# Causal attention with beacons, then a ReGLU FFN, on one core: scores issued three packed slabs at a time, output stores on another queue, block loads ordered behind the transpose of x

## The chip, the core and the metric

The kernel runs on one core of one Trainium2 chip. A core has five engines that run side by side and wait for each other through semaphores: TensorE (PE, matmuls; its weight loads are shown apart as PEld), VectorE (DVE), ScalarE (ACT), GpSimd (POOL) and SyncE (SP), which here issues DMAs. SP, ACT and POOL each have a queue of instructions in order; a DMA issued from a queue waits in it like any other instruction. The metric is the device time of one execution in microseconds (us). The kernel before takes 378.92 us, the median of 4 runs (378.21 to 380.38).

## The reference

```python
B, H, S, Nb, D = 8, 8, 576, 16, 64            # batches, heads, tokens, beacons, head width
k_all = concatenate([beacon_k, k], axis=2)    # 592 keys
v_all = concatenate([beacon_v, v], axis=2)
scores = (1 / sqrt(D)) * matmul(q, k_all.transpose(0, 1, 3, 2))
scores = where(causal, -1e9, scores)          # beacons are seen by all, tokens causally
a = exp(scores - scores.max(-1)); a /= a.sum(-1) + 1e-09
x = matmul(a, v_all)                          # then laid out as 4608 tokens x 512
gate, val = maximum(x @ w_gate, 0), x @ w_val # 512 -> 1536
out = (gate * val) @ w_out                    # 1536 -> 512
```

All inputs and the output are float32; the kernel computes in bfloat16 with float32 sums. It leaves out the maximum in the softmax (a flag computed at the end sends inputs out of range to a slow general path, which does not run with these inputs).

## The kernel before, in words

**Attention.** Keys are the partitions of a score tile, queries its columns. The 592 keys are five blocks of up to 128 rows (`kt`), and the queries fall into two groups: the first 368 rows (group 0) and the other 208 (group 1). The unit of work is a *burst*: one batch, one pair of heads (each head takes 64 of the 128 rows of PE, so two matmuls run side by side) and one query group. A batch has 4 x 2 = 8 bursts. The table `SLABS` lists, for each group, two *slabs* of up to 512 columns a head: which key block against which queries goes to which column. A slab is computed into one PSUM tile `s` of two banks, one bank a head; the pool `s_ps` has two such tiles.

A burst goes through `qk` (L331; the score matmuls, L339), `softmax` (L343; exp on ACT, L347, from PSUM to a bfloat16 tile `p`), `mask` (L350; DVE multiplies the diagonal part by a triangle, L358) and, one tick later, `av` (L360; the P·V matmuls, L378, whose last column gives the row sums; DVE normalises into `x`, L386 and L387). After the last head pair of a group, `x_turn` (L391) transposes x into `xT` by three or two DMAs on SP (L394).

**FFN.** `ffn_up` (L407) makes one 128-row slice of the hidden layer for one tile of tokens (368 or 208 wide): four gate matmuls (L411), relu on ACT (L414), four value matmuls (L417), the product on DVE (L425). `ffn_down` (L429) makes 128 rows of the output: twelve matmuls of 512 columns (L448), a copy by ACT to one of three output buffers `ob` (L451), and the store (L453). All PSUM tiles but the scores come from `f_ps`, a ring of four banks given out strictly in turn; the tile that takes a bank waits until its former content was read.

**Loads.** For batches 2 to 7 a `Load` fetches one block of k and q, or two blocks of v, into one of six staging buffers (DMAs on SP), POOL casts it to bfloat16 (L269, L282), and two DMA transposes on SP (L296) bring k and q to `kq`. `kq` and `vx` exist twice, for even and odd batches.

**Order.** It is written out by hand, and each engine runs its instructions in that order. After a start for batch 0, the loop of L657 goes through *ticks*, one burst of batches 1 to 7 in each (L633). A tick emits the burst's scores and exps, P·V of the burst of the tick before and, after a last head pair, the turn of x; then the casts and transposes of blocks loaded two and three ticks ago, the next block's load, and the masks. Then as many FFN pieces follow as a budget allows (L647): `ffn` is a list of pieces with an estimated cost in PE time, and `ready` says from which tick the x of a piece is there. Where the next piece is a narrow up (cost under 1) the second exp is placed after the first piece. Pieces left after the last tick follow at the end (L694).

Of the kernel before, what the change touches and what calls it, by code (L numbers as in the profile page):

```python
# [10 lines left out]
FP32 = mybir.dt.float32  # L11
# [131 lines left out]
def kernel(  # L143
# [15 lines left out]
    P = 128  # L159
# [169 lines left out]
        pass  # L329

    def qk(u):  # L331
        u.s, u.p = [], []
        kq = kqs[u.b % 2]
        for segs, cols, _ in SLABS[u.g]:
            s = s_ps.tile([P, 2, 512], FP32, name="s")
            for (kt, q0, n, c) in segs:
                for a in range(2):
                    rows = slice(a * D, (a + 1) * D)
                    T.matmul(s[:, a, c:c + n], kq[rows, 0, u.pi, kt * P:(kt + 1) * P],  # L339
                             kq[rows, 1, u.pi, Nb + q0:Nb + q0 + n], start=True, stop=True)  # L340
            u.s.append(s)

    def softmax(u, which=(0, 1)):  # L343
        for i in which:
            cols = SLABS[u.g][i][1]
            p = psb.tile([P, 2, 512], BF16, name="p")
            A.activation(p[:, :, :cols], u.s[i][:, :, :cols], AF.Exp, scale=scale)  # L347
            u.p.append(p)

    def mask(u, pool=False, which=(0, 1)):  # L350
        for i in which:
# [8 lines left out]
    def av(u):  # L360
        qt = QGROUPS[u.g]
        o = f_ps.tile([P, len(qt), 2, D + 2], FP32, name="f")
        blocks = {}
        for p, (segs, cols, _) in zip(u.p, SLABS[u.g]):
            for (kt, q0, n, c) in segs:
                for j, qi in enumerate(qt):
                    r0, rn = QROWS[qi]
                    if q0 <= r0 and r0 + rn <= q0 + n:
                        blocks[j, kt] = (p, c + r0 - q0)
        first = True  # L370
        for j, qi in enumerate(qt):
            kts = sorted(kt for (jj, kt) in blocks if jj == j)
            m = 80 if qi == 4 else P
            for a in range(2):
                for kt in kts:
                    p, c = blocks[j, kt]
                    kr = P if kt < 4 else KT4
                    T.matmul(o[:m, j, a, 0:D + 1], p[:kr, a, c:c + m],  # L378
                             vs[u.b % 2][:kr, kt, 2 * u.pi + a, 0:D + 1],
                             start=first, stop=(kt == kts[-1]), skip_group_check=True)  # L380
                    first = False
        parts = ((0, 3, P),) if u.g == 0 else ((0, 1, P), (1, 2, 80))
        for j0, j1, m in parts:
            i0 = qt[j0]
            r = rall[:m, u.b, u.pi, i0:i0 + j1 - j0]
            V.reciprocal(r, o[:m, j0:j1, :, D])  # L386
            V.tensor_mul(  # L387
                u.x[:m, i0:i0 + j1 - j0, u.pi * P:(u.pi + 1) * P].rearrange("p j (a d) -> p j a d", a=2),
                o[:m, j0:j1, :, 0:D], r.unsqueeze(3).to_broadcast([m, j1 - j0, 2, D]))
# [15 lines left out]
    hbs = {}  # L405

    def ffn_up(m0, mn, nf):  # L407
        def go():
            g = f_ps.tile([P, 512], FP32, name="f")
            for ki in range(KM):  # L410
                T.matmul(g[:, :mn], wg[:, ki, nf * P:(nf + 1) * P], xT[:, ki, m0:m0 + mn],  # L411
                         start=(ki == 0), stop=(ki == KM - 1))
            gs = fsb.tile([P, 512], FP32, name="g")
            A.activation(gs[:, :mn], g[:, :mn], AF.Relu)  # L414
            u = f_ps.tile([P, 512], FP32, name="f")
            for ki in range(KM):
                T.matmul(u[:, :mn], wv[:, ki, nf * P:(nf + 1) * P], xT[:, ki, m0:m0 + mn],  # L417
                         start=(ki == 0), stop=(ki == KM - 1))
            c = m0
            while c < m0 + mn:  # L420
                i = c // HB
                e = min((i + 1) * HB, m0 + mn)
                if i not in hbs:
                    hbs[i] = fsb.tile([P, NF, HB], BF16, name="hT")
                V.tensor_mul(hbs[i][:, nf, c - i * HB:e - i * HB], gs[:, c - m0:e - m0], u[:, c - m0:e - m0])  # L425
                c = e
        return go

    def ffn_down(i, ms):  # L429
        rows = slice(i * HB + ms * P, i * HB + (ms + 1) * P)  # L430

        def last():
            for n0 in (0, 256):
                o = f_ps.tile([P, 256], FP32, name="f")
                for nf in range(NF):
                    T.matmul(o, hbs[i][:, nf, ms * P:(ms + 1) * P], wo[:, nf, n0:n0 + 256],  # L436
                             start=(nf == 0), stop=(nf == NF - 1))
                ob = osb_p.tile([P, 256], FP32, name="ob")
                A.copy(ob, o)
                (A if n0 else nc.sync).dma_start(out[rows, n0:n0 + 256], ob)  # L440

        if (i + 1) * HB == n_tokens and ms == HB // P - 1:
            return last

        def go():
            o = f_ps.tile([P, d_model], FP32, name="f")
            for nf in range(NF):
                T.matmul(o, hbs[i][:, nf, ms * P:(ms + 1) * P], wo[:, nf, :],  # L448
                         start=(nf == 0), stop=(nf == NF - 1))
            ob = osb_p.tile([P, d_model], FP32, name="ob")  # L450
            A.copy(ob, o)  # L451
            oq = nc.sync if len(ffn) < 8 else OQ
            oq.dma_start(out[rows], ob)  # L453
        return go
# [14 lines left out]
        T.matmul(cnt_ps, ok, ones, start=True, stop=True)  # L469
        V.tensor_copy(cnt, cnt_ps)  # L470

    OQ = nc.sync
    NA, PRE = 2, 16
    tiles = []
    for b in range(B):
# [2 lines left out]
    with tc.manual_schedule():  # L478
# [13 lines left out]
        for b in range(B):  # L492
            for p, g in [(p, g) for g in range(2) for p in range(NP)]:
                u = Burst()
                u.b, u.pi, u.g, u.last = b, p, g, p == NP - 1
                bursts.append(u)

        def start(u):
# [76 lines left out]
                ffn += [(2.6, ffn_down(done, ms), m0 + mn) for ms in range(HB // P)]  # L575
                done += 1

        def next_ffn():
            ffn.pop(0)[1]()

        def burst(u):
            start(u)
# [45 lines left out]
        for b in range(2, B):  # L628
            kq = [Load("kq", b, t) for t in range(NKT)]
            vv = [Load("v", b, t, min(t + 2, NKT)) for t in range(0, NKT, 2)]  # L630
            pieces += [(b, x) for x in (kq[0], vv[0], kq[1], kq[2], vv[1], kq[3], kq[4], vv[2])]
        T0, GAP = 8, 1
        ticks = bursts[8:16] + [None] * GAP + bursts[16:] + [None]  # L633
        begin = {b: T0 + GAP + 8 * (b - 1) for b in range(2, B)}

        ready = {}
        for m0, mn in tiles:
            e = m0 + mn
            if e <= S:
                ready[e] = 0  # L640
                continue
            for s, u in enumerate(ticks, T0):
                if u and u.last and u.b * S + (368 if u.g == 0 else S) >= e:
                    ready[e] = s + 3
                    break

        def budget(s):  # L647
            best = 4.6 if s >= T0 + 8 else 2.4
            for r in sorted(set(ready.values())):
                if r > s:  # L650
                    best = min(best, sum(c for c, _, e in ffn if ready[e] < r) / (r - s))
            return best

        jobs = []
        prev = None
        spent, want = 0.0, 0.0
        for s, u in enumerate(ticks, T0):  # L657
            turn = u and u.b == 1 and u.g == 0 and not u.last
            if turn:
                pair_turn(c1, 1, u.pi + 1, 2, VA)  # L660
            late = False
            if u:
                late = not turn and ffn and ready[ffn[0][2]] <= s and ffn[0][0] < 1
                start(u)
                qk(u)
                softmax(u, (0,) if late else (0, 1))
            if prev:
                av(prev)
                if prev.last:
                    x_turn(prev)  # L670
            for at, f in [j for j in jobs if j[0] == s]:
                f()
            for _ in range(1):
                if pieces and s >= begin[pieces[0][0]] - 10:
                    b, x = pieces.pop(0)
                    x.issue()
                    jobs.append((s + 2, lambda x=x: x.cast(G)))
                    if x.kind == "kq":
                        jobs.append((s + 3, lambda x=x: x.turn()))
            rest = []  # L680
            if late:
                rest = [lambda: (softmax(u, (1,)), mask(u, which=(0,))), lambda: mask(u, which=(1,))]
            elif u:
                mask(u)
            prev = u
            want += budget(s)
            while ffn and ready[ffn[0][2]] <= s and spent + ffn[0][0] / 2 <= want:
                spent += ffn[0][0]
                next_ffn()
                if rest:  # L690
                    rest.pop(0)()
            for f in rest:
                f()
        while ffn:  # L694
            if len(ffn) == 10:
                range_flags()
# [38 lines left out]
```

## Time and profile before

| | us |
|---|---|
| median of 4 runs (lowest to highest) | 378.92 (378.21 to 380.38) |
| the profiled execution | 380.84 |
| its span, first to last instruction | 379.1 |
| PE busy, share of the span | 362.7, 96% |
| ACT busy | 204.7, 54% |
| DVE busy | 188.3, 50% |
| POOL busy | 73.0, 19% |
| granted PE clock, mean | 0.995 |

In rows of the profile, `f<-xT,wg` is an instruction that writes tile f from xT and wg; then come its shape, the count, and what it waited for. "SPq" is a DMA issued on the queue of SP. A time in brackets with an arrow is idle time of that engine before the instruction, and what ended it.

### The profile page before, as it was taken

Reading aid. Unit: us, or ns where it says so; the run is one execution under the profiler, and the core shown is the slowest. Engines: PE = TensorE matmul, PEld = TensorE weight load, DVE = VectorE, ACT = ScalarE, POOL = GpSimd, SP = SyncE. Lnnn points to the kernel's source line nnn. Section 1 sums busy time; section 2 is a strip of 40 time slices with the busy share of each in tenths; the row PEclk is TensorE's granted clock in tenths of the full one; section 3 lists DMA queues with packets and bytes.
Section 4 is the critical chain, followed back from the end, with each engine's and each line's share of the span. In section 5 each row is a group of like instructions: output and inputs, shape, how many; then the busy total and the mean of one; then the engine's idle time right before and its main releaser. Section 6 shows DMA issues by size and latency. Waiting matters only on the chain.

```text
span 379.1 us, 9589 instructions
## 1 busy us (share of the span) xinstructions
PE 362.7 (96%) x3757; PEld 237.3 (63%) x3757; DVE 188.3 (50%) x642; ACT 204.7 (54%) x372; POOL 73.0 (19%) x94
## 2 busy tenths in 40 slices
PE   2889998999999999999999999999999999999995
PEld 1547666567756686565596647865596647765763
DVE  3747458456635674265256633565165633552230
ACT  4755367546556665455465545565466545642321
POOL 5952023212221212121303122121202000000000
PEclk9989999999999999999999999999999999999999
DMA  8999999999989999898977496778959212001202
GB/s 145 178 200 207 179 208 176 192 188 119 175 158 216 131 153 163 201 166 143 220 123 158 87 228 150 133 134 149 210 100 162 42 55 84 15 14 39 85 31 88
DMA packets 158995, 53.12 MB, mean 140 GB/s; under 512 B 146528, under 2 KB 154464, under 8 KB 158944
## 3 DMA queue, kind: packets, MB, share of 16 engines
q1 hardware_dynamic: 149840, 45.24, 63.4%
q0 software_dynamic: 8816, 6.88, 11.9%
q8 instruction: 31, 0.51, 0.6%
q10 hardware_dynamic: 288, 0.33, 0.3%
q14 instruction: 20, 0.16, 0.2%
HBM read 38.47 MB, written 9.44 MB: 126 GB/s over the span
## 4 chain that ended last, share of the span: by engine, by line
PE 91%; DMA 3%; POOL 2%; ACT 1%; DVE 1%; issue 1%; DVEq 0%; ACTq 0%
PE f L417 24%; PE f L448 24%; PE f L411 24%; PE f L378 10%; PE s L339 7%; DMA wv<-in_moe_w_val_dram 2%; DMA stg<-in_k_dram 1%; ACT p L347 1%; PE f L436 1%; PE f L322 1%; POOL p L355 1%; DVE hT L425 0%; POOL cs L308 0%; POOL wg L507 0%; DVE p L358 0%
## 5 line engine op out<-in xcount | busy, mean ns | idle before, releaser
L425 DVE TENSOR_TENSOR hT<-g,f 128x208 bf16<-128x208 f32 (+14 forms) x288 | 92.8, 350 | 79.8 <-PE f L417 48.6
L417 PE MATMUL f<-xT,wv 128*128 128x368 bf16 (+1 forms) x768 | 126.1, 287 | 1.0 <-DMA wv<-in_moe_w_val_dram 0.5
L411 PE MATMUL f<-xT,wg 128*128 128x368 bf16 (+1 forms) x768 | 125.7, 286 | 1.0 <-ACT g L414 0.5
L414 ACT ACTIVATE g<-f 128x368 f32<-128x368 f32 (+1 forms) x192 | 78.9, 413 | 73.6 <-PE f L411 35.5
L347 ACT ACTIVATE p<-s 128x992 bf16<-128x992 f32 (+2 forms) x128 | 105.5, 864 | 19.9 <-PE s L339 19.8
L448 PE MATMUL f<-wo,hT 128*128 128x512 bf16 x420 | 94.3, 379 | 0.1
L417 PEld LDWEIGHTS <-wv 128*128 128x128 bf16 x768 | 71.4, 98 | 26.0 <-issue 0.9
L411 PEld LDWEIGHTS <-wg 128*128 128x128 bf16 x768 | 69.5, 98 | 21.2 <-issue 1.4
L448 PEld LDWEIGHTS <-hT 128*128 128x128 bf16 x420 | 40.1, 98 | 44.7
L282 POOL CAST c<-stg 128x1024 bf16<-128x1024 f32 (+1 forms) x30 | 31.9, 1063 | 133.1 <-DMA stg<-in_q_dram 133.1
L451 ACT COPY ob<-f 128x512 f32<-128x512 f32 x35 | 20.5, 585 | 67.5 <-PE f L448 66.2
L386 DVE RECIPROCAL rall<-f 128x2 f32<-128x2 f32 (+1 forms) x96 | 16.7, 174 | 76.9 <-PE f L378 76.4
L378 PEld LDWEIGHTS <-p 128*128 128x128 bf16 (+2 forms) x960 | 37.3, 108 | 13.7 <-issue 12.0
L378 PE MATMUL f<-vx,p 128*128 128x65 bf16 (+2 forms) x960 | 44.2, 200 | 0.8 <-DVE p L358 0.8
L358 DVE TENSOR_TENSOR p<-p,tri 128x160 bf16<-128x160 bf16 (+1 forms) x124 | 40.6, 346 | 4.5 <-ACT p L347 4.1
L387 DVE TENSOR_TENSOR x<-f,rall 128x128 bf16<-128x128 f32 (+1 forms) x96 | 36.3, 378 | 3.4
L339 PE MATMUL s<-kq 64*128 64x208 bf16 (+4 forms) x512 | 35.8, 261 | 1.8 <-ACT p L347 1.5
L269 POOL CAST vx<-stg 128x1024 bf16<-128x1024 f32 (+2 forms) x21 | 18.9, 898 | 76.1 <-DMA stg<-in_v_dram 73.9
L339 PEld LDWEIGHTS <-kq 64*128 64x128 bf16 x512 | 17.0, 97 | 19.5 <-issue 18.7
L325 DVE COPY kq<-f 128x192 bf16<-128x192 bf16 (+2 forms) x18 | 8.5, 507 | 5.3 <-PE f L322 4.6
L319 PE MATMUL f<-ident,c 64*128 64x64 bf16 x12 | 0.5, 234 | 6.3 <-DVE c L279 6.3
L322 PEld LDWEIGHTS <-cs 64*64 64x64 bf16 x264 | 3.6, 120 | 3.7 <-issue 3.6
(50 smaller groups left out, 53.6 us busy)
## 6 DMA issues: line engine op xcount, KB each, us to landing
out_dram<-ob SPq DMA_DIRECT2D x35, 256.0 KB, 3.3
stg<-in_v_dram SPq DMA_DIRECT2D x24, 256.0 KB, 4.6
stg<-in_k_dram SPq DMA_DIRECT2D x18, 256.0 KB, 3.9
stg<-in_q_dram SPq DMA_DIRECT2D x18, 256.0 KB, 4.2
stg<-in_v_dram SPq DMA_DIRECT2D x8, 224.0 KB, 3.4
wo<-in_moe_w_out_dram POOLq DMA_DIRECT2D x3, 512.0 KB, 14.5
stg<-in_k_dram SPq DMA_DIRECT2D x6, 224.0 KB, 3.7
stg<-in_q_dram SPq DMA_DIRECT2D x6, 224.0 KB, 3.7
```

Source lines behind the costliest of these rows:

```text
L282: cp(self.c[:n], self.st[:n])
L339: T.matmul(s[:, a, c:c + n], kq[rows, 0, u.pi, kt * P:(kt + 1) * P], kq[rows, 1, u.pi, Nb + q0:Nb + q0 + n], start=True, stop=True)
L347: A.activation(p[:, :, :cols], u.s[i][:, :, :cols], AF.Exp, scale=scale)
L358: V.tensor_mul(p[:, :, :m], p[:, :, :m], tri[:, :, :m])
L378: T.matmul(o[:m, j, a, 0:D + 1], p[:kr, a, c:c + m], vs[u.b % 2][:kr, kt, 2 * u.pi + a, 0:D + 1], start=first, stop=(kt == kts[-1]), skip_ ...
L387: V.tensor_mul(u.x[:m, i0:i0 + j1 - j0, u.pi * P:(u.pi + 1) * P].rearrange("p j (a d) -> p j a d", a=2), o[:m, j0:j1, :, 0:D], r.unsqueeze ...
L411: T.matmul(g[:, :mn], wg[:, ki, nf * P:(nf + 1) * P], xT[:, ki, m0:m0 + mn], start=(ki == 0), stop=(ki == KM - 1))
L414: A.activation(gs[:, :mn], g[:, :mn], AF.Relu)
L417: T.matmul(u[:, :mn], wv[:, ki, nf * P:(nf + 1) * P], xT[:, ki, m0:m0 + mn], start=(ki == 0), stop=(ki == KM - 1))
L425: V.tensor_mul(hbs[i][:, nf, c - i * HB:e - i * HB], gs[:, c - m0:e - m0], u[:, c - m0:e - m0])
L448: T.matmul(o, hbs[i][:, nf, ms * P:(ms + 1) * P], wo[:, nf, :], start=(nf == 0), stop=(nf == NF - 1))
L451: A.copy(ob, o)
```

## The change

Batch 0 and batch 1 keep their order. From batch 2 on, the ticks are replaced by 28 *phases* (in the code, a step that is a list). A batch's 8 bursts are cut into 14 slabs in place of 16: of two bursts of group 0, the two short second slabs (256 columns each) are packed into one of 512. A phase takes three slabs, across bursts and batches. Their scores are issued together at its start: the first slab into two tiles of the FFN ring `f_ps` (on loan, one bank a head, each with an exp of its own), the other two into `s_ps`. The first slab's exp follows at once, then one P·V whose last slab was in the phase before. The other exps are placed inside FFN pieces (`mid`, between relu and the value matmuls of an up, or between the matmuls and the copy of a down), at least 1.2 us of estimated PE time apart, and after such a piece comes another P·V that is due; a mask follows one FFN piece after its exp.

A phase counts as 3 x 8/14 = 1.71 ticks. Loads, casts and transposes have due times on that clock and are emitted between FFN pieces as it passes, but not while P·V of a last head pair is still to come in the phase (`held`), so that the turn of x stands before them on SP. The stores of the output, all but those of the last pieces, are issued by POOL in place of SP (`OQ`).

```diff
+    class Slab:
+        def __init__(self, segs, cols, spans):
+            self.segs, self.cols, self.spans = segs, cols, spans
+        def qk(self, s):
+            self.s = s
+            for u, (kt, q0, n, c) in self.segs:
+                kq = kqs[u.b % 2]
+                for a in range(2):
+                    rows = slice(a * D, (a + 1) * D)
+                    o = s[a] if isinstance(s, list) else s[:, a]
+                    T.matmul(o[:, c:c + n], kq[rows, 0, u.pi, kt * P:(kt + 1) * P],
+                             kq[rows, 1, u.pi, Nb + q0:Nb + q0 + n], start=True, stop=True)
+        def exp(self):
+            p = self.p = psb.tile([P, 2, 512], BF16, name="p")
+            if isinstance(self.s, list):
+                for a in range(2):
+                    A.activation(p[:, a, :self.cols], self.s[a][:, :self.cols], AF.Exp, scale=scale)
+            else:
+                A.activation(p[:, :, :self.cols], self.s[:, :, :self.cols], AF.Exp, scale=scale)
+            for u, seg in self.segs:
+                u.parts.append((p, (seg,)))
...
     def ffn_up(m0, mn, nf):
-        def go():
+        def go(mid=None):
...
             A.activation(gs[:, :mn], g[:, :mn], AF.Relu)
+            if mid:
+                mid()
             u = f_ps.tile([P, 512], FP32, name="f")
...
-    OQ = nc.sync
+    OQ = G
...
-        ticks = bursts[8:16] + [None] * GAP + bursts[16:] + [None]
+        steps = bursts[8:16] + [None] * GAP + bursts[16:8 + NT]
+        steps += [slabs[i:i + 3] for i in range(0, len(slabs), 3)] + [None]
+        widths = [W * len(e) if isinstance(e, list) else 1 for e in steps]
...
+            for i, sl in enumerate(e):
+                for u, _ in sl.segs:
+                    start(u)
+                sl.qk([f_ps.tile([P, 512], FP32, name="f") for _ in range(2)] if i == 0 else
+                      s_ps.tile([P, 2, 512], FP32, name="s"))
+            exps, masks = list(e), []
...
+            exp()
+            aver()
+            if not held():
+                passed(pos[s])
+            gone, was, room = 0.0, spent, max(want - spent, 0.1)
+            while fits():
+                c = ffn[0][0]
+                gone += c
+                mid = gone >= STEP
+                if mid:
+                    gone = 0.0
+                old = len(masks)
+                next_ffn(exp if mid else None)
+                spent += c
+                if old:
+                    masks.pop(0).mask()
+                if mid:
+                    aver()
+                if not held():
+                    passed(pos[s] + widths[s] * min((spent - was) / room, 0.99))
+            while exps:
+                exp()
+            while units:
+                aver()
+            for sl in masks:
+                sl.mask()
```

Here `exp()` takes the next slab of the phase and `aver()` the next P·V that is due, with the turn of x where it is the last; `passed(t)` emits the loads, casts and transposes due by t. The FFN may take 5.2 us of PE per tick's width where the limit was 4.6.

## The prediction

> **What bounds the kernel now.** I read the page first: busy time of each engine over the span.
>
> ```profile
> span 379.1 us, 9589 instructions
> PE 362.7 (96%) x3757; PEld 237.3 (63%) x3757; DVE 188.3 (50%) x642; ACT 204.7 (54%) x372; POOL 73.0 (19%) x94
> ```
>
> TensorE (PE) is busy for all but 16.4 us, and no other engine is above 54%. The second view, busy time by stretch, says where those 16.4 us lie (columns: stretch, length, then busy us of PE, weight loads, DVE, ACT and POOL with their instruction counts, then granted clock, DMA share and GB/s).
>
> ```profile
> 0.00:20.00 20.00, 11.56 (x184) 8.14 (x185) 10.44 (x29) 11.94 (x20) 14.30 (x30) 1.00 1.05 163
> 60.00:80.00 20.00, 19.20 (x228) 12.26 (x226) 12.93 (x42) 13.03 (x22) 5.42 (x5) 1.00 1.09 188
> 160.00:180.00 20.00, 20.00 (x185) 11.86 (x184) 11.54 (x42) 11.38 (x20) 3.73 (x4) 1.00 0.94 165
> 360.00:379.10 19.10, 14.39 (x102) 9.27 (x100) 3.15 (x10) 4.31 (x11) 0.00 (x0) 1.00 0.17 59
> ```
>
> Idle PE is in the start (before 80 us) and after the last matmul. From 80 to 360 us each stretch has 20.00 of 20.00. Batches 2 to 7 run there, and only for them does the change rewrite the order.
>
> Busy is not the same as streaming, so the third view is PE in order of time, where starts can be subtracted (start, duration, engine, line, operation, count).
>
> ```profile
> 78.45 0.79 PE L417 MATMUL f<-xT,wv 128*128 128x368 bf16 x4
> 79.07 0.79 PE L378 MATMUL f<-vx,p 128*128 128x65 bf16 x18
> 79.69 0.79 PE L411 MATMUL f<-xT,wg 128*128 128x368 bf16 x4
> ...
> 164.49 0.79 PE L417 MATMUL f<-xT,wv 128*128 128x368 bf16 x4
> 165.21 0.49 PE L339 MATMUL s<-kq 64*128 64x128 bf16 x6
> 165.64 0.80 PE L378 MATMUL f<-vx,p 128*128 128x65 bf16 x18
> 166.27 0.79 PE L411 MATMUL f<-xT,wg 128*128 128x368 bf16 x4
> ```
>
> Four 368-column matmuls take 0.62 us from start to start (0.156 each); in other rows four 208-column ones take 0.36 (0.089 each). The ratio is that of the columns, so they stream with no gap. One place does not: scores (L339) after an FFN group. The group at 164.49 should be over at 165.11, and the scores start at 165.21: 0.095 lost. The six score matmuls run in pairs on two 64-row halves, 752 columns a half, which at 0.089 per 208 is 0.32; the next group starts 0.43 later: about 0.10 lost again. P·V (L378) straight after FFN at 79.07 loses nothing (78.45 + 0.62). So entering and leaving the 64-row shape costs 0.19 us per group of scores. Over 80 to 360 us these two losses are nearly all that PE has beyond streaming.
>
> Here a rule speaks against me. The Trainium skill's "Perfetto Trace Analysis", section Identifying the Most-Contended Engine, says that matmul busy time is a bad measure of headroom and that the share of weight loads should be used. By it PE, at 63%, has a third of the span left, and a better order could win tens of us. By the starts above it has 0.19 us per group. I take the starts: a weight load (98 ns in its row) hides behind a 156 ns matmul and cannot fill the row.
>
> **The change part by part.**
>
> *Fewer groups of scores (gain).* Before, each of the 48 bursts of batches 2 to 7 issues its own scores: 48 groups. After, a batch has 14 slabs (two bursts of the first query group give three instead of four), 84 in all, issued three at a time: 28 groups. The score matmuls are the same in number and size, as are P·V and FFN. Some 21 P·V groups no longer follow scores but stand between FFN groups, which costs nothing by the row at 79.07. Sum: 20 groups x 0.19 = 3.8 us less on PE.
>
> *ACT.* The rows by shape:
>
> ```profile
> L347 ACT ACTIVATE p<-s 128x992 bf16<-128x992 f32 x64 | 63.9, 999 | 19.9 <-PE s L339 19.8
> L414 ACT ACTIVATE g<-f 128x208 f32<-128x208 f32 x96 | 32.9, 348 | 22.2 <-PE f L411 20.9 <-DVE hT L425 1.2
> L347 ACT ACTIVATE p<-s 128x512 bf16<-128x512 f32 x32 | 19.1, 596 | 0.0
> ```
>
> A pair of first-group bursts cost 2 x (0.999 + 0.596) = 3.19; three slabs cost 2 x 0.999 + some 1.03 = 3.03. But a slab on loan lies in two FFN buffers and needs two exps, at the 0.596 of the last row 1.19 instead of 1.0. Per batch that is -0.3 + 4.7 x 0.19 = +0.6 us of ACT in the 44 us that a batch lasts: nothing, while ACT is at 54%. What matters is bunching: all three slabs of a phase fall due in its first half.
>
> *The loan.* Scores now take two of the four FFN buffers. Taken step by step for a phase with 208-column FFN tiles, from the start of its scores: the first slab's scores are out at 0.2, its exps run from 0.4 to 1.0 and 1.6. PE does all scores until 0.63, P·V (12 matmuls, 0.37 plus the 0.1 exit) until 1.15, gate 1 until 1.5; value 1 takes the first lent buffer at 1.5 (free at 1.0) and gate 2 the second at 1.85 (free at 1.6). The loan itself holds nothing up, by a margin of 0.25. Then relu 1 (1.7 to 2.05), relu 2 (to 2.76), exp 2 (to 3.78), relu 3 (to 4.13), relu 4 (to 4.6), exp 3 (to 5.6), relu 5 (to 5.95). Gate 7 needs the buffer that relu 5 frees, and PE is there at 5.8: a stall of 0.2. Five phases consist mostly of 208-column tiles, three of them by half: 5 x 0.2 + 3 x 0.1 = 1.3 us. With 368-column tiles (1.25 us a step on PE against relu 0.48 + exp 1.0) ACT falls 0.23 behind per exp, twice, and the buffers absorb that: 0. Down-projections (2.6 us) give ACT more time: 0. From below: the stall could be 0, if the buffers cover it. From above: the crowded ticks of batch 1 lose up to 0.87 us each (0.47 of it in the row at 53.27 below), but ACT has kq copies there as well.
>
> *DVE.* 12 masks fewer (some 3 us in 188): hidden, 0. A mask collides with casts on POOL (rows in order of time):
>
> ```profile
> 63.02 1.04 POOL L269 CAST vx<-stg 128x1024 bf16<-128x1024 f32 x1 [0.97 <-PE f L411]
> 63.10 1.22 DVE L358 TENSOR_TENSOR p<-p,tri 128x480 bf16<-128x480 bf16 x1
> ```
>
> and PE, in the crowded ticks of batch 1, waited for ACT and for such a mask:
>
> ```profile
> 53.27 0.52 PE L411 MATMUL f<-xT,wg 128*128 128x208 bf16 x4 [0.47 <-ACT g L414]
> 64.38 0.27 PE L378 MATMUL f<-vx,p 128*128 128x65 bf16 x3 [0.52 <-DVE p L358]
> ```
>
> The mask took 1.22 us beside the cast instead of 0.44 (the mean of its group, 13.2 us over 30). After the change P·V comes a whole phase after most of its masks, so a mask 0.8 late reaches no PE instruction except through the products (L425) behind it: 0, at most 0.4 in a few phases.
>
> *Stores on POOL.* 32 of the 37 stores move (the last three row blocks stay on SP and ACT). On SP they held others up:
>
> ```profile
> SPq L453 <- ACT ob L451: 74.8, 22, 31.2
> ```
>
> That is SP time; SP is busy without a gap from 53 to 95 us, so two stores fewer there (0.81 and 1.19 us) bring the third kq block of batch 2 some 2 us forward. It was issued at 78.47 and ended at 81.0, for scores at 84.78; the new order asks for them one FFN up (1.25 us) earlier. Both together: 0. On POOL a store is queued with the casts: behind a store that waits for its ACT copy stands a cast, behind that a kq transpose, which by the order has six ticks until its use. Behind a cast that waits for its block stands a store: copy 0.59 + issue 0.77 + landing 5.2 (the longest of these stores; the weights' 256 KB on this queue took 6.1 to 6.6) is 6.6 to 8.0, against three output buffers x 2.6 = 7.8 until reuse. Worst case 0.2 to 1.2 once per run of four stores, on ACT, and PE has 2.6 us of work: 0.
>
> The rule against this part: the skill's "SBUF — State Buffer", in its box on DVE blocking DMA, says that a DMA issued from POOL cannot write its descriptors while DVE runs an operation that takes the shared port in a two-port mode, such as a float32 copy. By it every store could be late by one DVE copy (0.76 us in this trace). In batches 2 to 7 DVE runs products, masks and reciprocals and no copies, so this trace gives the rule nothing to act on; and the 0.76 would fit the slack above. I take 0.
>
> *Block loads behind the turn of x.* The same loads, casts and transposes, at the same distance of nine ticks before use. Where P·V of the last head pair is still due, they wait for it; x's transposes (2 or 3 at 1.25 us, landing 2.7) then stand first. The shortest distance is the phase where the turn opens the phase and its rows are used at the next one's first up: five ups of 1.25, scores, P·V, 7.8 us, against 0.9 (normalising) + 2.5 + 2.7 = 6.1. 0.
>
> Sum: -3.8 + 1.3 = -2.5 us. The profiled run took 380.84 (span 379.1 and 1.74 around it, untouched): 378.3. It lies 1.9 above the median shown; the same 2.5 off 378.92 gives **376.4 us**.
>
> **The rivals.**
> *Clean.* No stall on 208-column tiles, and a little less waiting at 50 to 65 us: 378.9 - 3.8 - 0.3 = 374.8. For it: the stretch now has no stalls of over 0.1 beyond the shape changes. Against it: the walk above.
> *No change.* The switches go, but stalls of 0.136 per phase (28 x 0.136 = 3.8) take their place, from bunched exps and late products together: 378.9. For it: at 199.84 an up already waits 0.09 for a product.
> *Slower.* The loan is late: if ACT has a backlog at the start of a phase (a copy of 0.59, then two exps of 0.6), value 1 or gate 2 waits for the lent buffer in each phase, whatever its tiles. It decides above 0.20 per phase; at 0.25: 28 x 0.25 - 3.8 = +3.2, 382.1. For it: the margin is 0.25 with an idle ACT, and a phase after a down-projection has it not. Against it: only one phase with 208-column tiles follows such a one directly.
>
> **How the numbers follow.** Likeliest 0.46 (375.4 to 377.0 by itself), clean 0.14, no change 0.22, slower 0.18. Half a per cent (1.9 us) is about what a measurement tells from no change. Faster 0.60, same 0.22, slower 0.18. Range: down to 374.2 (all 3.8 and a little of the start), up to 381.0, which takes in no change and the near part of slower.
>
> **What would show it.** Right: 28 groups of scores of 10 to 16 matmuls after 80 us, FFN after P·V without a gap, end of matmuls some 2.5 us earlier, PE waits for ACT's g of about 0.2 in the 208-column phases. Wrong: waits of PE's FFN groups for ACT's p (the loan), for ACT's g in every phase, for transposed x, or idle PE anywhere from 80 to 360 us.

## The result, and the profile after

The changed kernel takes 378.42 us (median of 38 runs, 375.89 to 381.31) against 379.15 for the kernel before, re-timed beside it (59 runs, 378.03 to 382.97): a ratio of 0.9974, interval 0.996 to 0.9988. That is faster by 0.26%, about 1.0 us, where I had forecast 2.5. The new times are inside my range, but nearer to no change than to my number. They also spread more at the low end: before, the middle of the runs lay close to the lowest; now there are 2.5 us between.

The profiled run lies near the low end of these times: 376.50 us. The page of the changed kernel:

```profile
span 374.7 us, 9601 instructions
PE 357.5 (95%) x3757; PEld 239.4 (64%) x3757; DVE 191.8 (51%) x630; ACT 204.4 (55%) x388; POOL 90.1 (24%) x126
```

Against 379.1 that is 4.4 us less, but the two profiles do not start alike: the first scores of batch 1 begin at 50.77 us in the one of before and at 48.15 here, in a part that the change does not rewrite (between 20 and 40 us the granted clock was 0.91 in the first and 1.00 in the second). Over twenty profiles of this study that moment lies between 48.0 and 50.8, whatever the kernel. From there to the end the spans are 328.3 and 326.5. I call this *the rest* below, and compare profiles by it. The change itself shows as 1.8 us in this pair.

TensorE (PE) in order of time, two places of the changed kernel in the first phases of batch 2 (start, duration, engine, line, operation, count):

```profile
88.08 0.39 PE L356 MATMUL f<-kq 64*128 64x128 bf16 x4
88.30 0.59 PE L356 MATMUL s<-kq 64*128 64x128 bf16 x8
88.83 0.54 PE L413 MATMUL f<-vx,p 128*128 128x65 bf16 x12
...
90.27 0.52 PE L454 MATMUL f<-xT,wv 128*128 128x208 bf16 x4
90.63 0.53 PE L413 MATMUL f<-vx,p 128*128 128x65 bf16 x12
91.00 0.52 PE L446 MATMUL f<-xT,wg 128*128 128x208 bf16 x4
...
93.53 0.52 PE L454 MATMUL f<-xT,wv 128*128 128x208 bf16 x4
93.88 0.52 PE L446 MATMUL f<-xT,wg 128*128 128x208 bf16 x4
94.33 0.53 PE L454 MATMUL f<-xT,wv 128*128 128x208 bf16 x4
```

Three slabs of scores stand together at 88.08. P·V inside the FFN costs nothing: 90.27 + 0.36 = 90.63. In the phase of 208-column tiles, where I had walked ACT through and found a stall of 0.2, one value group starts 0.09 late (93.88 to 94.33 is 0.45 in place of 0.36), behind a product that had waited for ACT. So the order does on PE what it should. By stretch:

```profile
80.00:100.00 20.00, 20.00 (x222) 15.36 (x221) 12.80 (x43) 13.62 (x29) 4.76 (x5) 1.00 1.12 147
100.00:120.00 20.00, 18.73 (x172) 10.46 (x170) 6.24 (x25) 9.54 (x17) 6.76 (x9) 1.00 1.15 211
160.00:180.00 20.00, 20.00 (x162) 11.80 (x159) 10.88 (x37) 11.45 (x20) 2.62 (x3) 1.00 0.90 143
```

Between 100 and 120 us PE now idles for 1.27 us, where it had been busy throughout. PE and SP in that stretch, changed kernel (the bracket is idle time and what ended it):

```profile
101.06 3.03 SPq L296 DMA_TRANSPOSE kq<-c  x2
...
102.83 0.56 DVE L422 TENSOR_TENSOR x<-f,rall 128x384 bf16<-128x384 f32 x1
...
104.14 0.58 SPq L254 DMA_DIRECT2D stg<-in_k_dram  x1
104.76 0.69 SPq L255 DMA_DIRECT2D stg<-in_q_dram  x1
...
105.56 5.15 SPq L429 DMA_TRANSPOSE xT<-x  x3
...
112.69 0.78 PE L446 MATMUL f<-xT,wg 128*128 128x368 bf16 x4 [0.95 <-DMA xT<-x]
...
116.17 0.44 PE L356 MATMUL s<-kq 64*128 64x128 bf16 x4 [0.33 <-DMA kq<-c]
```

The P·V whose x is turned is issued on PE at 102.04, in 12 matmuls, and DVE has written x at 103.39 (102.83 + 0.56). The three transposes of x (L429) start only at 105.56, 2.17 us later, behind two k/q transposes and two block loads of batch 3. They last 5.15 us, and the FFN's first gate on that x waits. At 116.17 the first scores of batch 3 wait for their keys. The same turn in the kernel before:

```profile
97.16 4.09 SPq L296 DMA_TRANSPOSE kq<-c  x2
101.29 0.58 SPq L254 DMA_DIRECT2D stg<-in_k_dram  x1
101.92 0.58 SPq L255 DMA_DIRECT2D stg<-in_q_dram  x1
...
105.44 0.56 DVE L387 TENSOR_TENSOR x<-f,rall 128x384 bf16<-128x384 f32 x1
...
106.03 4.96 SPq L394 DMA_TRANSPOSE xT<-x  x3
```

Here x was ready at 106.00, and the turn started 0.03 us later: not late. Counted from the first scores of batch 1 in each, x is ready at 55.2 us in both kernels. The turn started at 55.3 before (106.03 - 50.77) and starts at 57.4 now, with one more pair of k/q transposes and one more block of batch 3 ahead of it. So what is late is SP, not x.

### The profile page after: what moved, and what is told of

Same layout as the page of the kernel before. It is cut to its first block, busy times and chain, and to the rows that moved or that the text cites. A ratio compares the mean times of both kernels' runs of the same rounds, so it can differ in the third digit from the quotient of the medians.

```text
span 374.7 us, 9601 instructions
## 1 busy us (share of the span) xinstructions
PE 357.5 (95%) x3757; PEld 239.4 (64%) x3757; DVE 191.8 (51%) x630; ACT 204.4 (55%) x388; POOL 90.1 (24%) x126
## 4 chain that ended last, share of the span: by engine, by line
PE 85%; DMA 7%; SPq 2%; POOL 1%; ACT 1%; issue 1%; DVE 1%; ACTq 0%; POOLq 0%; DVEq 0%
PE f L454 24%; PE f L446 24%; PE f L485 21%; PE f L413 9%; PE s L356 3%; DMA stg<-in_q_dram 2%; PE f L356 2%; DMA wv<-in_moe_w_val_dram 2%; DMA stg<-in_v_dram 2%; PE s L339 1%; DMA kq<-c 1%; SPq L296 1%; PE f L473 1%; DVE hT L462 1%; ACT p L381 1%
## 5 line engine op out<-in xcount | busy, mean ns | idle before, releaser
L365 ACT ACTIVATE p<-s 128x992 bf16<-128x992 f32 (+2 forms) x56 | 53.8, 966 | 0.0
L492 POOL DMA_DIRECT2D out_dram<-ob x32 | 17.3, 542 | 134.9 <-ACT ob L490 125.7
L413 PEld LDWEIGHTS <-p 128*128 128x128 bf16 (+2 forms) x960 | 38.3, 107 | 9.9 <-issue 6.0
L413 PE MATMUL f<-vx,p 128*128 128x65 bf16 (+2 forms) x960 | 43.4, 199 | 0.2 <-DVE p L393 0.2
L363 ACT ACTIVATE p<-f 128x496 bf16<-128x496 f32 (+2 forms) x56 | 28.7, 567 | 7.6 <-PE f L356 7.6
L372 DVE TENSOR_TENSOR p<-p,tri 128x160 bf16<-128x160 bf16 (+1 forms) x72 | 28.9, 405 | 0.4 <-ACT p L365 0.4
L381 ACT ACTIVATE p<-s 128x992 bf16<-128x992 f32 (+2 forms) x32 | 26.1, 865 | 4.9 <-PE s L339 4.8
L356 PEld LDWEIGHTS <-kq 64*128 64x128 bf16 x384 | 13.9, 94 | 10.1 <-issue 9.0
L356 PE MATMUL s<-kq 64*128 64x208 bf16 (+4 forms) x256 | 16.2, 249 | 0.3 <-DMA kq<-c 0.3
```

The source lines that it names most:

```text
L356: T.matmul(o[:, c:c + n], kq[rows, 0, u.pi, kt * P:(kt + 1) * P], kq[rows, 1, u.pi, Nb + q0:Nb + q0 + n], start=True, stop=True)
L365: A.activation(p[:, :, :self.cols], self.s[:, :, :self.cols], AF.Exp, scale=scale)
L372: V.tensor_mul(self.p[:, :, :m], self.p[:, :, :m], tri[:, :, :m])
L413: T.matmul(o[:m, j, a, 0:D + 1], p[:kr, a, c:c + m], vs[u.b % 2][:kr, kt, 2 * u.pi + a, 0:D + 1], start=first, stop=(kt == kts[-1]), skip_ ...
```

## The experiments

The theory: the order's gain is there in full on PE, and most of it is given back by DMAs that come late in the stretch from 70 to 145 us. The rivals: the stores on POOL cost it; ACT is crowded in the phases. In each block a ratio is to the kernel before on the same chip.

**Leaving the loads out, in both kernels.** From batch 2 on the k, q and v of batches 0 and 1 are used again. With the loads go their casts on POOL and their k/q transposes on SP; all other work stands. The same holds below wherever a batch's loads are said to be left out.

```diff
-        for b in range(2, B):      # where the blocks of batches 2 to 7 are listed (before), or given due times (changed)
+        for b in range(0):
```

> The kernel before without the block loads, casts and k/q transposes of batches 2 to 7 (they compute on batch 0's and 1's k, q and v; all other work is the same, so the output is wrong there). Both theories: TensorE does not wait for these loads in the kernel before, so the time stays within 1 us of before (some 0.5 less in the ticks of batch 1, where casts meet masks).

> The changed kernel with the same loads left out (output wrong from batch 2 on). Theory (late DMA): with no loads the turn of x is never late; the full 3.8 us of the order appears: 3 to 4 us below the kernel before without loads, so near 374.5 to 375.5, with a narrow spread. Rival (stores, or crowded ACT): the loss is not in loads, and the difference to the kernel before without loads stays near 1 us.

Measured: 378.40 us for the kernel before without loads (ratio 0.9974, 0.9962 to 0.9986) and 374.86 for the changed one (0.989, 0.9865 to 0.9914). Without loads the new order is worth 3.54 us by the medians (3.2 by the two ratios, whose intervals leave some 0.9 us either way); with them about 1.0. The rest (first scores of batch 1 to the end) is 328.4 and 324.6: 3.8 apart. With its loads the kernel before has 328.3, so they cost it nothing there in that profile. The changed kernel loses 1.9 in its profile, and by the medians 378.42 - 374.86 = 3.6 in all, of which the kernel before loses about 1.0 too (379.40 - 378.40; no profile shows where). Two things this pair does not separate: what of the loads costs the time (packets, SP or casts), and what the stores do without loads, since they stand on POOL in the one kernel and on SP in the other.

**Batch 3's loads alone.** Batch 3 uses another batch's k, q and v.

```diff
-        for b in range(2, B):
+        for b in (2, 4, 5, 6, 7):
```

> The changed kernel without the block loads, casts and k/q transposes of batch 3 alone (it computes on batch 1's there; output wrong). Theory (SP is late once, around 100 to 116 us, because the blocks of batches 2 and 3 come on top of each other): most of the loss is gone, 375.5 to 376.5. Rival (masks held out by casts in every batch): 1/6 of the 3.6 us, so near 377.8.

Measured: 375.40 (0.9892, 0.9871 to 0.9914), rest 325.1. Leaving out one batch of six gives back all that leaving out six did, within the noise: the loss does not recur in each batch.

**Is a group of scores worth 0.19 us?** Phases of two slabs, with the loads left out.

```diff
-        steps += [slabs[i:i + 3] for i in range(0, len(slabs), 3)] + [None]
+        steps += [slabs[i:i + 2] for i in range(0, len(slabs), 2)] + [None]
```

> The changed kernel without the loads of batches 2 to 7 (output wrong), in phases of two slabs in place of three: 42 groups of scores in place of 28. Theory (0.19 us per group): 14 x 0.19 = 2.7 us above the changed kernel without loads (374.9), so near 377.5. Rival (the 3.5 us between the two orders without loads come from something else, such as fewer ticks with crowded ACT): within 1 us of 374.9.

Measured: 378.08 (0.9953, 0.9934 to 0.9972), 3.2 us over three slabs without loads: 0.23 per group over 14 groups. The two were timed on different chips; by their ratios it is 2.4 us, and by the rests (327.2 against 324.6) 2.6: 0.17 and 0.18 per group. The price per group holds; ACT has less bunching with two slabs and is no help.

**The stores.** First alone in the kernel before, then taken back in the changed one.

```diff
-    OQ = nc.sync
+    OQ = G        # kernel before; the reverse in the changed kernel
```

> The kernel before with its 32 stores on POOL and nothing else changed. Theory (late DMA): the new order saves 3.8 us on TensorE in batches 2 to 7, and some 2 to 3 us of it are given back between 45 and 120 us, where blocks and transposes come late; the stores have a small part in it, through block loads of batch 1 and 2 that start some 3 us sooner and casts that meet masks: +0.3 to +0.8 us against before, and the same spread as before. Rival (stores): POOL's stores hold up casts or output buffers, and that is where the gain went: +1.5 us or more, and a wider spread.

> The changed kernel with its stores back on SP. Theory (late DMA): SP is the queue that is late around 100 to 116 us, and stores in it that wait for ACT make the turn of x later still: slower than the changed kernel by 0.5 to 2 us, near 379 to 380. Rival (stores): without POOL's stores the full gain appears: 375.5 to 376.5.

Measured: 380.23 alone (1.0026, 1.0016 to 1.0036), and 380.43 for the changed kernel with stores on SP (1.0021, 1.0003 to 1.004). By the ratios, stores on POOL are a loss of 1.0 us in the old order, more than I expected, and a gain of about 2 in the new one. Where the old order loses, by the profile of the kernel before with its stores on POOL:

```profile
230.61 1.05 POOL L282 CAST c<-stg 128x1024 bf16<-128x1024 f32 x1
...
231.24 1.50 DVE L358 TENSOR_TENSOR p<-p,tri 128x160 bf16<-128x160 bf16 x1
...
231.59 1.05 POOL L269 CAST vx<-stg 128x1024 bf16<-128x1024 f32 x1
...
233.08 0.52 PE L417 MATMUL f<-xT,wv 128*128 128x208 bf16 x4 [0.50 <-DVE hT L425]
```

Two casts that had queued behind a store run back to back; the mask between them takes 1.50 us (its group's mean is 0.27 before) and ends as they end, and a value matmul waits for the product behind it. It happens again at 274.5. With stores on SP in the new order PE waited 3.4 us for transposed x in that profile, twice. So the stores are not what ate the gain.

**The changed kernel once more,** with no edit, for a second profile of it.

> The changed kernel once more, for a second profile, since its times spread over 5.4 us. Theory (late turn of x): a time near its median, 378.4, and in the profile idle TensorE before gates of the FFN between 90 and 145 us that wait for transposed x, 1 to 3 us in sum, or a gap of like size at value matmuls that wait for a product. Rival (crowded ACT): waits of gates for ACT's relu buffers in many phases.

Measured: 378.16 us (0.9965, 0.9942 to 0.9988); its profiled run took 377.49, with a rest of 325.7. PE again waited 1.0 us for the turned x, at the same place near 112 us, and no wait for a crowded ACT has taken its place. So that wait is no accident of one profile.

**The order on SP.** Loads not held behind the turn of x:

```diff
-                return any(u.last for u in units)
+                return False
```

> The changed kernel with the holding back taken out: due loads are emitted in a phase even if P·V of a last head pair is still to come, so that up to three DMAs stand before the turn of x on SP. Theory (turn of x late once, near 107 us, behind loads): later still there, and perhaps in other batches, 379 to 381. Rival (holding costs, since the loads it delays are late): 377 to 378.

Measured: 378.46 (0.9962, 0.9937 to 0.9987), no different from the changed kernel: the rival is nearer. In its profile the turn started 2.43 us after its x was ready, the first gate on x waited 1.05 us and batch 3's scores 0.68. Holding back acts when an instruction is emitted; here SP is behind the emission, and loads emitted a phase earlier already stand ahead of the turn.

v loads (L242, L244) of batches 2 and 3 on POOL, or of batch 3 alone:

```diff
                 b, t0, t1 = self.key
+                if b in (2, 3):            # second run: b == 3
+                    dma = G.dma_start
```

> The changed kernel with the v loads of batches 2 and 3 (10 DMAs at some 0.5 us of SP each) issued by POOL. Theory (SP is late): SP is some 5 us further on at 105 us, the turn of x is on time, 376.0 to 377.2. Rival (the DMA engines are full, whichever queue issues): no change, 378 to 379; a third way: POOL's queue, casts behind loads, makes it worse, 379 to 380.

> The changed kernel with the v loads of batch 3 alone (5 DMAs) on POOL. In the run with batches 2 and 3 the wait at 107 us was gone, but the turn of x of batch 1 came 1.7 us late at 76 us. Theory (SP's length of queue before the turn at 107 us): the first without the second, 376.5 to 377.5. Rival (full DMA engines): 378 to 379.

Measured: 379.40 (0.9983, 0.9962 to 1.0005) and 377.54 (0.9946, 0.9923 to 0.9969). Waits of PE in the profile of the first:

```profile
PE f L448 <- DMA xT<-x: 2.7, 1, 2.7
```

This one begins at 70.6 us, at the turn of batch 1, while the one near 111 us is gone. (The expectation of the second run has it as 1.7 us at 76; the trace shows 2.7.) SP issued that turn at 63.77, as early as the changed kernel does (63.76), but the transposes landed 4.2 to 6.3 us after their issue in place of 2.8 to 3.9: this wait came from the transfers, not from the queue of SP. The time is in the range of the third way, but POOL's queue was not seen to be its cause. In the second run PE waited 1.5 for x at 90 and 0.4 for keys at 117. Each run relieves one place and finds the next.

Batch 3's scores out of batch 2's last phase, and batch 3's loads a tick later:

```diff
-        steps += [slabs[i:i + 3] for i in range(0, len(slabs), 3)] + [None]
+        cuts = list(range(0, 14, 3)) + list(range(14, len(slabs), 3)) + [len(slabs)]
+        steps += [slabs[i:j] for i, j in zip(cuts, cuts[1:])] + [None]
```

> The changed kernel with a phase of two slabs at the end of batch 2, so that batch 3's first scores are not taken into batch 2's last phase: 29 phases, and batch 3 and its loads come 1.1 ticks later on the emission's clock, where they were before the change. Theory (batch 3's blocks are asked of SP and the DMA engines some 8 us earlier than before the change, on top of batch 2's turn of x): +0.2 for the phase, the late DMAs gone, 375.6 to 376.8. Rival (lateness is set by something else than batch 3's time): 378 to 379.

```diff
-                load(pos[enters[b]] - {2: 9.5, 3: 9}.get(b, BB) + i, 8 * b + i, x)
+                load(pos[enters[b]] - {2: 9.5, 3: 8}.get(b, BB) + i, 8 * b + i, x)
```

> The changed kernel with batch 3's loads due one tick later (8 in place of 9 ahead), its scores where they were. Theory: fewer loads stand before the turn of x at 107 us, but its key blocks come closer to the scores at 116 us, so the one wait is exchanged in part for the other: 377 to 378.5. Rival (the loads only have to leave the turn's way): 376 to 377.

Measured: 378.18 (0.9955, 0.9936 to 0.9973) and 379.97 (1.0004, 0.9982 to 1.0026). Both put batch 3's loads back to where they were before the change, and in both profiles the turn near 103 us starts 0.03 us after its x is ready: so the earlier loads are what made it late. Yet the first missed its forecast: the wait near 111 us is gone, but x was late at 131 us (0.8), and casts holding masks out cost 1.4 in one wait at 230. In the second, PE's longest wait in the profile after the start:

```profile
PE s L356 <- DMA kq<-c: 3.5, 1, 3.5
```

One tick of delay and the keys are 3.5 us late: the loads had no slack to give. That was worse than either theory had it, and the wait is not the whole price. By stretch, around the wait that ends at 118.11 (the granted clock is the third number from the end):

```profile
114.00:118.00 4.00, 0.59 (x11) 0.43 (x11) 0.54 (x1) 1.06 (x2) 1.04 (x1) 0.88 1.23 207
118.00:122.00 4.00, 3.89 (x30) 2.37 (x30) 0.82 (x4) 0.81 (x2) 1.60 (x2) 0.50 1.36 185
122.00:126.00 4.00, 4.00 (x36) 2.78 (x35) 2.25 (x8) 2.03 (x4) 1.04 (x1) 0.77 1.02 191
```

From 117.0 on TensorE ran at half its clock for 6.8 us, 5.7 of them after the wait; half of that, some 2.9 us, is lost on top of the 3.5. The rest of this run, 330.8, is 6.2 over that of the changed kernel without loads.

**What is short: SP's time or the DMA engines?** Loads of batches 2 and 3 as 2 KB runs in place of 256 B, the same bytes and as many DMAs, read from other rows of the same tensors.

```diff
+        if b in (2, 3) and s1 - s0 > Nb:
+            n = s1 - s0
+            return src[b].rearrange("h (u r) d -> (h u) r d", r=8)[:n]
         return src[b, :, s0:s1].rearrange("h p d -> p h d")
```

> The changed kernel where the k, q and v loads of batches 2 and 3 read the same number of bytes as 2 KB runs in place of 256 B (from the wrong places, so the output is wrong there); the same DMAs stand on SP. Theory (the DMA engines, full of short packets between 20 and 116 us, are what is short): 375.2 to 376.4, with no waits for transposed x. Rival (SP's queue time, above all 1.25 us per transpose): not under 377.5. A gain in between says both.

Measured: 376.03 (0.9919, 0.9898 to 0.994), and no wait for x or keys in the profile. SP stands idle from 101.3 us until the x of the turn is ready at 104.6. By stretch (the last three columns are clock, DMA share, GB/s):

```profile
80.00:100.00 20.00, 19.81 (x218) 14.94 (x216) 12.30 (x40) 13.13 (x28) 5.16 (x6) 1.00 0.78 185
100.00:120.00 20.00, 20.00 (x188) 11.65 (x184) 8.54 (x28) 10.97 (x20) 6.52 (x9) 1.00 0.81 175
```

The DMA share falls from 1.12 and 1.15 to 0.78 and 0.81, while the two stretches move as much as before (185 and 175 GB/s against 147 and 211). All casts, transposes and stores are still there, so it is not the casts. By this run the packets are most of what is short. One thing goes with the run length here: each block now reads the same rows of its tensor, and what that alone does was not run. SP is not apart from this: from 50 to 120 us its DMA instructions add up to 65.7 us of 70 in the changed kernel and to 58.8 here. In the kernel before it is 64.8: SP was about as full then. Over these 70 us a transpose of x held SP for 1.58 us on average in the changed kernel at a DMA share of 1.14, for 1.41 before at 1.00, and for 1.35 here at 0.82.

**Versions that might keep more.** Batch 1's x transposed on PE, and stores on ACT's queue, and both:

```diff
                     av(u)
-                    if u.last:
+                    if u.b == 1:
+                        due.append(u)          # x_turn_pair(u) one step later
+                    elif u.last:
                         x_turn(u)
```

> The changed kernel with batch 1's x transposed on TensorE (20 transposes of some 0.05 us, and eight copies on DVE) in place of five DMA transposes: +1.0 us on TensorE, 6.3 us of SP and the packets of five transposes freed between 66 and 90 us. Theory (SP and DMA engines have no slack from 50 to 116 us): late DMAs shrink by 2 us or more, so 376.5 to 377.6 in all. Rival (lateness arises after 100 us on its own): 379 to 379.8.

```diff
-    OQ = G
+    OQ = A
```

> The changed kernel with its stores issued by ACT (0.36 us each by the last store's row, 32 x 0.36 = 12 us of ACT, at 55% of the span). Theory: POOL's casts are free of the stores and SP too, so casts no longer meet masks in bunches and block loads move up a little: 377.2 to 378.2. Rival (ACT is crowded in the phases): ACT falls behind after down-projections, 379 or more.

> Both edits together, batch 1's x on TensorE and stores on ACT: if their gains add, 376 to 377; if the late DMAs only move on, 378 or more.

Measured: 377.43 (0.9948, 0.9927 to 0.9968), 378.76 (0.9987, 0.9965 to 1.0009) and 378.50 (0.9982, 0.9965 to 0.9999). On ACT the stores gain nothing; in that profile:

```profile
PE f L485 <- ACT p L363: 2.0, 1, 2.0
```

ACT stood for 4.8 us with a store next in its queue (what held the store is not shown), the exps of a loaned slab behind it, and a down-projection waited for the lent buffer. This is the rival that I had called slower, once in a run, and only with another queue in play.

In full the first edit collects such a unit in `due` and calls `x_turn_pair(o, V.tensor_copy)` for it in the next step, after that step's scores and before its loads and FFN pieces. The last two runs add v loads on POOL to it (of batch 3, then of batches 2 and 3, by the lines shown above):

> Batch 1's x on TensorE and batch 3's v loads on POOL. If the two gains add: 376.3 to 377.2. If lateness only moves on: 377.4 or more, no better than either.

> The same with the v loads of batches 2 and 3 on POOL. The turn of x that this made late at 70 us is no longer a DMA, so the harm seen with it should be gone: 376 to 377.2. If POOL's queue itself is the harm (casts behind loads): 378 or more.

Measured: 377.73 (0.9945, 0.9925 to 0.9965) and 377.36 (0.994, 0.9919 to 0.996). The gains did not add. These two, the v loads of batch 3 on POOL and batch 1's x on PE alone lie at 0.994 to 0.995, with intervals that overlap: four ways to about 0.3% under the changed kernel. No one of them is shown to be best, and three of the four intervals overlap the changed kernel's own (0.996 to 0.9988); the fourth touches it.

## Why the prediction was wrong

*Fewer groups of scores, -3.8:* right. 3.2 to 3.5 by the times without loads, 3.8 by the profiles' rest, and 0.17 to 0.23 per group at 14 more groups.

*The loan and ACT, +1.3:* too much. The loan held nothing up, as I had walked it. In the trace without loads, eight value groups of 208 columns between 85 and 342 us start 0.06 to 0.09 late, 0.6 us in sum; the kernel before without loads has seven such places with 0.5 in sum. So this term is some 0.1 us: most of the delay is there without the new order too.

*DVE, 0 to 0.4 in a few phases:* the mechanism was right, and one such wait of 1.4 us was seen in the run with batch 3 later. In the changed kernel's own profile PE waited 1.2 for products in all, half of it in the first tick of batch 1, and in the phases one value group came 0.3 late (273.43).

*Stores on POOL, 0:* the step was too simple. In the old order they cost 1.0 us, with two waits of 0.5 at casts in bunches; in the new one they save about 2. That SP has no time for them fits the 3.4 us of waits for x with them on SP. (The 1.2 of my worst case does not follow from its own figures: 8.0 against 7.8 is 0.2.)

*Block loads behind the turn of x, 0:* this step failed, and by its size decides the result. The new order gains 3.5 without loads and 1.0 with them, so the term was 2.5 us, not 0 (2.2 by the ratios). I had counted the distance from load to use in ticks, found it the same nine, and looked for the shortest way from turn to use in the order as it is emitted. But I had the row that speaks against it in my own text: SP busy without a gap from 53 to 95 us, with a DMA share of 1.09 in the row of 60 to 80 us. A queue that is behind does not act at the place where its instruction is emitted. What changed is when batch 3's loads are asked for. Scores issued three slabs at a time take batch 3's first slab into batch 2's last phase, so that the due times of its loads lie 1.1 ticks earlier; that puts one more block and one more pair of transposes ahead of the turn, which starts 2.17 us after its x is ready. With the loads put back it starts at once.

My walk had 6.1 us from the end of P·V to transposed x: 0.9 for normalising, 2.5 for the transposes, 2.7 for landing. The changed kernel's profile has 10.1 (102.57 to 112.69): 0.8 for normalising, 2.2 in SP's queue, 5.15 for three transposes where I had reckoned with two at 1.25, and 2.0 from the last one's end to the gate. PE was there at 111.74. The check that was missing: the turn's start on SP and the first use of its x, both in us, with the backlog in.

That late turn is not the whole 2.5. It cost 1.0 us in each of two profiles. Eight runs with all loads in place and their packets unchanged had it start at once, and took 377.36 to 379.97, with waits elsewhere or none that I can name. What gave the 2.5 back was taking batch 3's loads away, or lengthening the packets of two batches.

My sum was 3.8 - 1.3 = 2.5; the runs say 3.5 - 2.5 = 1.0. The two errors partly cancelled, by luck: with the ACT term at the 0.1 that was measured, my forecast would have been 3.7 and further off.

The rule that spoke against me (the Trainium skill's "Perfetto Trace Analysis", section Identifying the Most-Contended Engine) names MFU, the kernel's arithmetic as a share of the peak, beside the share of weight loads. I left that half out, and no run here measures it. The share of weight loads was 62 to 64% in every profile, while PE was busy for 20.00 of 20.00 us in most stretches, and no run came out as much as 5 us under the kernel before: the starts were the right thing to go by.

What is not settled: the changed kernel's own profiles (376.50, and a second at 377.49 with the same wait of 1.0 for x) are both faster than its median. Waits for x or keys at 70, 90, 111, 116, 131 and 134 us were seen in profiles of its variants, and the runs without batch 3's loads or with long packets lose both the waits and the wide spread (374.87 to 376.96 and 375.18 to 376.92, though in 6 runs each against 38). That the slower runs of the changed kernel itself have these waits is inferred from this, and not seen.

## What to carry to other kernels

Where PE streamed, what was left were its changes of shape: count them, and price one from two starts in the trace. When a new order brings consumers forward or packs them tighter, check every queue that feeds them in microseconds and with its backlog, not in places of the order; here a queue without gaps and a DMA share near 1 were the sign that nothing could be asked sooner. Take the suspected supply out in both kernels: it prices the order and the supply separately in two runs.

## What the runs showed of the hardware that I had not expected

- The same bytes as 2 KB runs in place of 256 B for two batches' loads took the DMA share from 1.15 to 0.81 in a stretch and 2.4 us from the kernel (378.42 to 376.03; 2.1 by the ratios), with the place read changed too.
- A DMA transpose does not hold SP for a fixed time: 1.2 to 1.3 us each where SP and the DMA engines had little else to do, up to 2.41 for one of the three that start at 106.03 in the kernel before, and 1.58 on average between 50 and 120 us in the changed kernel.
- Long waits of TensorE cost more than themselves. The four longest after 60 us were 1.96, 2.00, 2.71 and 3.52 us, in the runs with stores on SP, stores on ACT, v loads of two batches on POOL, and batch 3's loads a tick later. Within 1.2 us of the end of each the granted clock stood at half, for 3.4 us in the first three and for 6.8 in the last, where it began before the wait was over. By an estimate from this, 3.4 us at half speed lose 1.7 us of work. After the waits of 0.84 to 1.48 us it did not fall; a wait between 1.48 and 1.96 was not seen.
- A mask of DVE beside two casts of POOL, one after the other, took 1.50 us in place of 0.27 in the kernel before with stores on POOL, and one of 256 columns 2.44 in place of 0.34 in the run with batch 3 later. Both ended 0.1 us after the second cast.
